# Two mixture-of-experts layers behind windowed attention on one core: the seam of the layers rearranged

## Chip, cores, metric

One core of a Trainium2 chip. The metric is the device time of one execution in microseconds, as the median of several runs. Traces come from one profiled execution. Engines: PE (TensorE), DVE (VectorE), ACT (ScalarE), POOL (GpSimd), SP (SyncE, which here only issues DMAs).

## What is computed

```
x = attention(q, k, v)                    # 2304 tokens x 512, windowed heads
for layer in (1, 2):                      # 8 experts, one expert for each token
    e    = argmax(x @ w_gate [+ modality_bias])
    gate = softmax(logits)[e]             # layer 1 also multiplies by a sigmoid
    x    = gate * (relu(x @ w1[e]) @ w2[e])     # w1[e]: 512x1024, w2[e]: 1024x512
```

The second layer's expert of a token can be known only from the first layer's result for it.

## The kernel before

Attention runs first (lines up to 540). Each mixture layer then works in **slots**: a slot is 128 tokens of one expert. A float32 value is split into a float16 high and low part (`hi`, `lo`), so one product becomes three matmuls. A slot in `moe` is:

- `mm1`, twice 48 matmuls of 128 columns (`ph0`, `ph1`; `ph<-xT,wb`, L824), for the two halves of the hidden units; `hsplit` turns each half into `hh` (ACT, L832) and `hl` (DVE, L833);
- 24 matmuls of 512 columns (L891): 16 on `hh`, then 8 on `hl`, into `py` (in slots 0 and 1 into `pya0`, `pya1`);
- `post.out` of the slot before: ACT scales `py` into a tile `y` (layer 2: L1139) and POOL scatters it to `out` by an indirect DMA (L1140). Layer 2 has two such tiles, `y[s % 2]`, so slot 2 writes the tile of slot 0 again. `post.out(2, py)` stands at the start of slot 3, ahead of slot 3's `hsplit` on ACT.

Slots 0 and 1 use an expert that is guessed early, with rows gathered early (`xsA`). What comes after them is known when `sort` has counted the tokens of each expert. `sort` is a generator that is stepped from hooks: step 1 is a chain on DVE, step 2 two small matmul groups, steps 3 and 4 a chain on DVE with parts on POOL and ACT (POOL makes `bs` and `bm`, DVE from them `ob` and `A`), step 5 the 54 small matmuls `pidx` (L690, L691), step 6 the row numbers `idx` (DVE cast, L695) and three gathers on POOL (L796, slots 2 to 4), step 7 the table `tab` of experts on DVE (L706 to L729), with the transposing DMAs `xT` (L803) and the loads of slot 3's weights (L88: eight pieces of 512 KB into `raw`, by SP, which must first read the table, L812), steps 8 and 9 the gates (`Bgb` on POOL, `pg` on PE, `flb`, `gsb`).

`first_splits(FIRST[0..3])` makes float16 weights `wb` of slot 3 out of `raw`: four parts, each an ACT instruction on 128x2048 (L96) and a DVE instruction (L101); each part, once split, lets SP load two pieces for slot 4 into the same place.

Nothing is scheduled by a program: the order on every engine is that in which the code issues. `plan` maps (slot, hook) to what is issued there: hook 0 is the slot's start, 1 within `ph0`, 2 behind it, 3 behind `hsplit(0)`, 4 within `ph1`, 5 behind `hsplit(1)`, 6 after 12 of the 24 wide matmuls, 7 the slot's end. Layer 2's sort (`so2`) also needs layer 1's last slot: `post1.out(None)`, eight transposes on PE with a DVE copy (`turn`), and `router(None)`.

In layer 1 `post1.out` writes `y16p[s % 2]`; the second of these tiles lies in `lotmp`, which earlier holds gathered rows that the DMA `xsA<-lotmp` reads. Its last 16 columns are cleared on POOL at L936, ahead of POOL's part of layer 1's sort.

Of the kernel before, what the change touches and what calls it, by code (L numbers as in the profile page):

```python
# [20 lines left out]
N, DM, E, F = 2304, 512, 8, 1024  # L21
# [3 lines left out]
P = 128  # L25
# [11 lines left out]
SX1, SX2, SW, SWR1, SWR = 2.0 ** 5, 2.0 ** 10, 2.0 ** 6, 2.0 ** 6, 2.0 ** 4  # L37
# [3 lines left out]
FIRST = ['B0:4 D0:4', 'B4:8 D4:8', 'B8:12 D8:12', 'B12:16 D12:16']  # L41
# [8 lines left out]
def fused(ctx, tc, qk, vw, wr1, w1a, w2a, mid, wr2, mbias, w1b, w2b, cf, c16, cbs, cms, cib, out, dbg=None):  # L50
    nc = tc.nc
# [71 lines left out]
    identh = const.tile([P, P], F16, name="identh")  # L123
# [18 lines left out]
    lg2 = const.tile([P, NSLOT, E], F32, name="lg2")  # L142
# [129 lines left out]
    with ExitStack() as actx:  # L272
# [208 lines left out]
        def stR(n):  # L481
# [3 lines left out]
            for j in range(5):  # L485
                c0 = 64 + P * j - (64 if odd else 0)
                for k, (a, w) in enumerate(((0, 0), (0, 1), (1, 0))):
# [10 lines left out]
                          lambda nm, sh, dt=F32: ap1.tile([P] + [CA1 if k < 0 else k for k in sh], dt, name=f"fs_{nm}"),  # L498
# [77 lines left out]
    m1 = ctx.enter_context(tc.tile_pool(name="m1", bufs=1))  # L576

    ctx.enter_context(tc.manual_schedule())
    pp = ctx.enter_context(tc.tile_pool(name="pp", bufs=1, space=PSUM))
    wb2 = m1.tile([P, 2, 8192], F16, name="wb2")  # L580
    xgb = [m1.tile([P, ROW], F16, name=f"xg{i}") for i in range(3)]
    xg2 = [m1.tile([P, ROW], F16, name=f"xgA{i}") for i in range(KA)]
    xsb = [m1.tile([P, 8, P], F16, name=f"xT{i}") for i in range(3)]
# [9 lines left out]
    vt, gt = nc.vector, nc.gpsimd  # L593
# [14 lines left out]
    def sort(nm, lg, nt, inv, fe, ea, tab, scale, og, extra, gscale, start):  # L608
# [5 lines left out]
        sh = [P, nt, E]  # L614
# [68 lines left out]
        for a in range(0, nt, ACH):  # L683
            n = min(ACH, nt - a)
# [45 lines left out]
        eql = T("eql" + nm, [NSLOT])  # L730
        v.tensor_scalar(eql, iota_t, nlast, None, op0=ALU.is_equal)
        start.eql, start.nlast = eql, nlast
        start.transpose(KA)
        start.weights(KE, range(0, 3), always=True)
        start.transpose(KA + 1)
        start.weights(KE, range(3, 8), always=True)
# [39 lines left out]
        g = m1.tile([P, NSLOT], F32, name=f"gs{nm}")  # L776
# [8 lines left out]
    def moe(w1, w2, tab, src, parts, post, start, wpair):  # L785


        xg, xs, regs, turns = {}, {i: xsA[i] for i in range(KA)}, {}, {}
        py = pp.tile([P, DM], F32, name="py", tag="py")
        pys = [pp.tile([P, DM], F32, name=f"pya{i}", tag=f"pya{i}") for i in range(KA)]  # L790
# [8 lines left out]
        def x_transpose(s):  # L799
            if s >= NSLOT:  # L800
                return
            g = xg.pop(s)
            nc.sync.dma_start(xsb[s % 3], g[:, 0:8 * P], transpose=True)  # L803
            xs[s] = xsb[s % 3]
            post.gathered(s, g)

        def weights(s, pieces=range(8), always=False):
            if s >= NSLOT:
                return
            if s not in regs:  # L810
                regs.pop(s - 2, None)
                regs[s] = (nc.sync.value_load(tab[0:1, 0, s:s + 1], min_val=0, max_val=E - 1),  # L812
                           None if always else nc.sync.value_load(tab[0:1, 1, s:s + 1], min_val=0, max_val=1))
            load_raw(w1, w2, regs[s][0], cond=regs[s][1], pieces=pieces)
# [20 lines left out]
        def slot(s):  # L835
# [40 lines left out]
            if s >= KA:  # L876
                x_transpose(s + 2)
# [20 lines left out]
                post.router(s - 2)  # L898
            hook(7)

        start.gather, start.transpose, start.weights, start.pys = gather, x_transpose, weights, pys
        start.first_splits = lambda o: splits(wpair[KE % 2], o, lambda k: weights(KE + 1, k))
        for s in range(NMIN):
            slot(s)
# [14 lines left out]
        return r  # L919

    class Start:
        def hook(self, s, k):
            for f in self.plan.get((s, k), ()):
                f()

    def run(gen, n=1):
        def go():
            for _ in range(n):
                next(gen, None)
        return go  # L930


    y16s = m1.tile([P, ROW], F16, name="y16")
    y16p = [y16s, lotmp[:, 0:520].bitcast(F16)]
    for t in (*y16p, xg2[0]):
        gt.memset(t[:, 2 * DM:], 0.0)  # L936
    wr2h = m1.tile([P, 2, 4, E], F16, name="wr2h")
    fes2 = first_expert("b", lg2[:, 0:1, :], lambda: pp.tile([P, E], F32, name="pfe2", tag="pyt"), fe2)
# [30 lines left out]
    class Start1(Start):  # L969
        def fields(self, g, inv, ex):  # L970
            self.g, self.inv = g, inv

            md = ex[:, 0]
            nmod = m1.tile([P, NSLOT], F32, name="nmod")
            gt.tensor_scalar(nmod, md, -1.0, 1.0, op0=ALU.mult, op1=ALU.add)
            bm = m1.tile([P, NSLOT, E], F32, name="bm", tag="tmp")
            sh = [P, NSLOT, E]
            gt.tensor_tensor(bm, mbt[:, 0, :].unsqueeze(1).to_broadcast(sh), nmod.unsqueeze(2).to_broadcast(sh), op=ALU.mult)
            gt.tensor_tensor(lg2, mbt[:, 1, :].unsqueeze(1).to_broadcast(sh), md.unsqueeze(2).to_broadcast(sh), op=ALU.mult)
            gt.tensor_tensor(lg2, lg2, bm, op=ALU.add)  # L980
# [19 lines left out]
    start1 = Start1()  # L1000

    class Post1:
# [38 lines left out]
        def router(self, s):  # L1041
            pl = pp.tile([P, E], F32, name="plg", tag="plg")
            yT = self.yT[0 if s is None else s % 2]
            k = 0
            for c in range(4):
                for a, b_ in ((c, 0), (c, 1), (4 + c, 0)):
                    nc.tensor.matmul(pl, yT[:, a, :], wr2h[:, b_, c, :], start=k == 0, stop=k == 11)
                    k += 1
            if s is None:
                tmp = m1.tile([P, NSLOT, E], F32, name="lgt", tag="tmp")  # L1050
                sh = [P, NSLOT, E]
                vt.tensor_tensor(tmp, pl.unsqueeze(1).to_broadcast(sh), start1.eql.unsqueeze(2).to_broadcast(sh), op=ALU.mult)
                vt.scalar_tensor_tensor(out=lg2, in0=tmp, scalar=1.0 / (SX2 * SWR), in1=lg2, op0=ALU.mult, op1=ALU.add)
            else:
                vt.scalar_tensor_tensor(out=lg2[:, s, :], in0=pl, scalar=1.0 / (SX2 * SWR), in1=lg2[:, s, :], op0=ALU.mult, op1=ALU.add)

    post1 = Post1()
    so1 = sort("a", lg1[:, :, 0:8], NT, None, fe1, early[0], tabs[0], 1 / (SX1 * SWR1), lg1[:, :, 8:16], [midf], SX2 / (SX1 * SW * SW), start1)
    fs2 = []

# [14 lines left out]
    def at(s, k, *f):  # L1075
        plan.setdefault((s, k), []).extend(f)
# [7 lines left out]
    for i in range(NSLOT - NMIN):  # L1084
        at(0, 3, lambda i=i: start1.zero(i))
    at(1, 5, lambda: start1.first_splits(FIRST[0]))
    at(2, 0, first_out(post1, start1, 0), lambda: start1.first_splits(FIRST[1]))
    at(2, 3, lambda: start1.first_splits(FIRST[2]))
    at(2, 5, first_out(post1, start1, 1), lambda: start1.first_splits(FIRST[3]))
    at(3, 7, start1.last)  # L1090
# [7 lines left out]
    py1 = moe(w1a, w2a, tabs[0], x_dram, (0, 1, 4, 5, 2, 3, 6, 7), post1, start1, wbuf)  # L1098
# [4 lines left out]
    ilast = m1.tile([P, 1], I32, name="ilast")  # L1103

    class Start2(Start):
        def fields(self, g, inv, ex):
            self.g = g
            oobf = m1.tile([P, NSLOT], F32, name="oobf")
            self.oob = m1.tile([P, NSLOT], I32, name="oob")
            gt.tensor_scalar(oobf, inv, float(OOB), None, op0=ALU.mult)  # L1110
            gt.tensor_copy(self.oob, oobf)
            for i in sorted(post2.rows):
                post2.index(i)
# [34 lines left out]

    start2, post2 = Start2(), Post2()
    so2 = sort("b", lg2, NSLOT, start1.inv, fe2, early[1], tabs[1], 1.0, None, [], 1 / (SX2 * SW * SW), start2)  # L1150
    plan = start2.plan = {}
    at(0, 0, lambda: post1.out(None, py1))
    at(0, 1, lambda: post1.transposes(None))
    at(0, 2, lambda: post1.router(None))
    at(0, 3, run(so2))
    at(0, 6, run(so2))
    at(0, 7, run(so2, 2))
    at(1, 5, run(so2, 2))
    at(1, 7, run(so2))
    at(2, 0, run(so2))  # L1160
    at(2, 2, run(so2))
    at(2, 0, lambda: start2.first_splits(FIRST[0]))
    at(2, 3, first_out(post2, start2, 0), lambda: start2.first_splits(FIRST[1]))
    at(2, 5, first_out(post2, start2, 1), lambda: start2.first_splits(FIRST[2]), lambda: start2.first_splits(FIRST[3]))
    at(3, 7, start2.last)
    py2 = moe(w1b, w2b, tabs[1], y_dram, range(8), post2, start2, [wb2, wbuf[1]])
    post2.out(None, py2)
# [60 lines left out]
def _build(arrays, dbg=None):  # L1228
    import concourse.bacc as _bacc
    nc = _bacc.Bacc("TRN2", target_bir_lowering=False, num_devices=1)  # L1230
    args = []
    for n in _ORDER:
        a = arrays[f"in_{n}"]
        args.append(nc.dram_tensor(f"in_{n}", a.shape, mybir.dt.from_np(a.dtype), kind="ExternalInput").ap())
    args.append(nc.dram_tensor("out_0", (N, DM), F32, kind="ExternalOutput").ap())
    d = {k: nc.dram_tensor(f"dbg_{k}", sh, dt, kind="ExternalOutput").ap() for k, (sh, dt) in (dbg or {}).items()}
    with tile.TileContext(nc) as tc:  # L1237
        fused(tc, *args, dbg=d)
    return nc
# [9 lines left out]
```

## Time and profile before

| | |
|---|---|
| median of 3 runs | 668.83 us (668.12 to 671.66) |
| profiled execution | 672.37 us, of which the trace's span is 670.5 |
| PE matmul busy | 595.0 us, 89% |
| DVE / ACT / POOL busy | 358.2 / 268.1 / 201.2 us |
| mean granted TensorE clock | 0.948 of full |

A busy PE includes matmuls at the lower clock. The first layer's slots begin at about 167 us, the second layer's at 442 us.

### The profile page before, as it was taken

Reading aid. Unit: us, or ns where it says so; the run is one execution under the profiler, and the core shown is the slowest. Engines: PE = TensorE matmul, PEld = TensorE weight load, DVE = VectorE, ACT = ScalarE, POOL = GpSimd, SP = SyncE. Lnnn points to the kernel's source line nnn. Section 1 sums busy time; section 2 is a strip of 40 time slices with the busy share of each in tenths; the row PEclk is TensorE's granted clock in tenths of the full one; section 3 lists DMA queues with packets and bytes.
Section 4 is the critical chain, followed back from the end, with each engine's and each line's share of the span. In section 5 each row is a group of like instructions: output and inputs, shape, how many; then the busy total and the mean of one; then the engine's idle time right before and its main releaser. Section 6 shows DMA issues by size and latency. Waiting matters only on the chain. (4 is left out here: it accounts for less than half of the span.)

```text
span 670.5 us, 19530 instructions
## 1 busy us (share of the span) xinstructions
PE 595.0 (89%) x7432; PEld 458.8 (68%) x7432; DVE 358.2 (53%) x656; ACT 268.1 (40%) x397; POOL 201.2 (30%) x327
## 2 busy tenths in 40 slices
PE   3888988942998899999999999979699999999994
PEld 2777877842865777777777768766558677686772
DVE  4599897758849535954849722239251110113560
ACT  4577776632355224823638411111332111113451
POOL 2467766715360211101102410003622122121320
PEclk9699998955899999999999999978989999999998
DMA  9999999996399965997877772200995252332921
GB/s 206 222 221 218 246 235 251 256 271 193 89 312 326 322 161 140 349 299 147 218 224 226 192 116 69 43 21 19 288 347 136 49 97 63 83 86 71 324 54 44
DMA packets 109573, 121.29 MB, mean 181 GB/s; under 512 B 73104, under 2 KB 77968, under 8 KB 108433
## 3 DMA queue, kind: packets, MB, share of 16 engines
q1 hardware_dynamic: 103776, 101.97, 59.9%
q0 software_dynamic: 5280, 17.13, 8.6%
q8 instruction: 62, 1.02, 0.6%
q10 hardware_dynamic: 400, 0.72, 0.5%
q14 instruction: 55, 0.44, 0.2%
HBM read 214.11 MB, written 18.22 MB: 346 GB/s over the span
## 5 line engine op out<-in xcount | busy, mean ns | idle before, releaser
L824 PEld LDWEIGHTS <-wb 128*128 128x128 f16 x4032 | 231.1, 99 | 15.5 <-issue 8.8
L824 PE MATMUL ph<-xT,wb 128*128 128x128 f16 x3648 | 210.2, 219 | 2.7 <-DMA xT<-xg 1.9
L833 DVE SCALAR_TENSOR_TENSOR hl<-ph,hh 128x512 f16<-128x512 f32 x84 | 57.7, 688 | 163.8 <-ACTq L847 158.1
L891 PE MATMUL py<-wb,hh 128*128 128x512 f16 x608 | 139.5, 382 | 4.3 <-ACT hh L832 4.3
L101 DVE SCALAR_TENSOR_TENSOR wb<-raw,wb 128x1024 f16<-128x1024 f32 (+1 forms) x80 | 103.0, 1325 | 27.2 <-ACT wb L96 27.0
L891 PEld LDWEIGHTS <-hh 128*128 128x128 f16 x672 | 64.4, 99 | 76.2 <-ACT hh L832 5.4
L832 ACT ACTIVATE hh<-ph 128x512 f16<-128x512 f32 x84 | 50.1, 596 | 139.0 <-PE ph L824 138.6
L96 ACT ACTIVATE wb<-raw 128x1024 f16<-128x1024 f32 (+1 forms) x80 | 87.0, 1133 | 18.8 <-DMA raw<-in_w1b 7.8
L891 PE MATMUL py<-wb,hl 128*128 128x512 f16 x304 | 73.0, 384 | 0.0
L891 PEld LDWEIGHTS <-hl 128*128 128x128 f16 x336 | 33.2, 99 | 40.9 <-issue 1.9
L1140 POOL DMA_INDIRECT out<-y,idx x18 | 18.0, 1001 | 124.5 <-ACTq L847 93.2
L420 PE MATMUL po<-v,pT 128*96 128x65 f32 x384 | 41.4, 262 | 0.4 <-DMA v<-in_vw 0.3
L420 PEld LDWEIGHTS po<-v,pT 128*96 128x96 f32 x384 | 38.2, 177 | 0.8 <-DMA v<-in_vw 0.7
L796 POOL DMA_INDIRECT xg<-x_dram,idxaa x23 | 27.2, 1183 | 29.0 <-DMA xT<-xg 19.9
L1139 ACT ACTIVATE y<-py,gsb 128x512 f32<-128x512 f32 x16 | 11.0, 687 | 57.4 <-PE py L891 57.4
L361 DVE TENSOR_REDUCE M<-ps 96x4 f32<-96x512 f32 x48 | 31.6, 679 | 4.0 <-PE ps L360 3.8
L359 PE MATMUL ps<-kh,qs 128*96 128x128 f16 x192 | 30.5, 235 | 3.3 <-ACT kh L315 3.0
L824 PE MATMUL ph<-xsA,wb 128*128 128x128 f16 x384 | 26.5, 238 | 7.7 <-issue 4.9
L359 PEld LDWEIGHTS <-qs 128*96 128x96 f16 x192 | 25.0, 135 | 12.0 <-DVE qs L340 6.9
L318 DVE SCALAR_TENSOR_TENSOR kl<-qk,kh 128x608 f16<-128x608 f32 x32 | 29.0, 909 | 5.6 <-ACT kh L315 5.3
L360 PE MATMUL ps<-kl,qs 128*96 128x128 f16 x192 | 30.1, 234 | 1.8 <-DVE kl L318 1.8
L355 PE MATMUL ps<-mS,identb 96*96 96x512 bf16 x48 | 20.4, 426 | 11.3 <-DMA mS<-in_cbs 8.8
(397 smaller groups left out, 746.9 us busy)
## 6 DMA issues: line engine op xcount, KB each, us to landing
raw<-in_w1a SPq DMA_DIRECT2D x95, 512.0 KB
raw<-in_w2a SPq DMA_DIRECT2D x92, 512.0 KB
raw<-in_w1b SPq DMA_DIRECT2D x75, 512.0 KB
raw<-in_w2b SPq DMA_DIRECT2D x72, 512.0 KB
qk<-in_qk SPq DMA_DIRECT2D x16, 608.0 KB
v<-in_vw SPq DMA_DIRECT2D x16, 390.0 KB
qk<-in_qk SPq DMA_DIRECT2D x16, 304.0 KB
y_dram<-y SPq DMA_DIRECT2D x11, 260.0 KB
```

Source lines behind the costliest of these rows:

```text
L96: nc.scalar.activation(wb[:, 0, s], raw[:, s], AF.Copy, scale=SW)
L101: nc.vector.scalar_tensor_tensor(out=wb[:, 1, s], in0=raw[:, s], scalar=SW, in1=wb[:, 0, s], op0=ALU.mult, op1=ALU.subtract)
L318: nc.vector.scalar_tensor_tensor(out=kls[n][:, h], in0=krs[n][:, h], scalar=SQK, in1=khs[n][:, h], op0=ALU.mult, op1=ALU.subtract)
L359: nc.tensor.matmul(ps[:, j, :], st, kh[:, h, QT * i:QT * i + 128], start=False, stop=False, skip_group_check=True)
L360: nc.tensor.matmul(ps[:, j, :], st, kl[:, h, QT * i:QT * i + 128], start=False, stop=j == 3, skip_group_check=True)
L361: nc.vector.tensor_reduce(out=Ms[n][:, 4 * g:4 * g + 4], in_=ps, axis=AX.X, op=ALU.max)
L420: nc.tensor.matmul(po[:, i, :], pT[:, NQ * h + i, :], v[:, h, i, :], start=True, stop=True)
L796: nc.gpsimd.indirect_dma_start(t, None, src, bass.IndirectOffsetOnAxis(start.idx[:, s:s + 1], 0))
L824: nc.tensor.matmul(ph[:, j, :], w[:, c, fs], xT[:, parts[c + i], :], start=k == 0, stop=k == 47, skip_group_check=True)
L832: nc.scalar.activation(hs, ph, AF.Relu)
L833: nc.vector.scalar_tensor_tensor(out=hl[:, 4 * g:4 * g + 4, :], in0=ph, scalar=0.0, in1=hs, op0=ALU.max, op1=ALU.subtract)
L891: nc.tensor.matmul(to, a, w, start=k == 0, stop=k == len(ops) - 1)
```

## The change

Nothing is computed differently; instructions move and one kind is replaced.

- Layer 2: `post1.transposes(None)` is issued in hook 0 of slot 0 and `router(None)` in hook 1, with step 1 of the sort right behind it, ahead of the slot's `hsplit`. The router's update touches only the 10 slots that can be the last one.
- Step 5 moves from hook 5 of slot 1 to hook 6, and step 9 from hook 2 of slot 2 to hook 5.
- Slot 2's rows are turned by eight PE transposes into PSUM and an ACT copy (`x_turned`), not by the DMA of L803.
- `first_splits(0)` comes at hook 3 of slot 2, the other three at hook 5; both `post2.out` of slots 0 and 1 move to hook 7, behind them.
- Layer 1: the clearing of the part of `lotmp` moves from the start to hook 0 of slot 2.

```diff
-        start.transpose(KA)
+        (start.turned if start.by_pe else start.transpose)(KA)
...
+        def x_turned(s):
+            g = xg.pop(s)
+            pt = pp.tile([P, 8, P], F16, name="pxt", tag="pyt")
+            for c in range(8):
+                nc.tensor.transpose(pt[:, c, :], g[:, c * P:(c + 1) * P], identh)
+            nc.scalar.copy(xsb[s % 3], pt)
+            xs[s] = xsb[s % 3]
+            post.gathered(s, g)
...
-    for t in (*y16p, xg2[0]):
+    for t in (y16s, xg2[0]):
         gt.memset(t[:, 2 * DM:], 0.0)
...
-    at(2, 0, first_out(post1, start1, 0), lambda: start1.first_splits(FIRST[1]))
+    at(2, 0, first_out(post1, start1, 0), lambda: start1.first_splits(FIRST[1]), lambda: gt.memset(y16p[1][:, 2 * DM:], 0.0))
...
-    at(0, 0, lambda: post1.out(None, py1))
-    at(0, 1, lambda: post1.transposes(None))
-    at(0, 2, lambda: post1.router(None))
-    at(0, 3, run(so2))
+    at(0, 0, lambda: post1.out(None, py1), lambda: post1.transposes(None))
+    at(0, 1, lambda: post1.router(None), run(so2))
     at(0, 6, run(so2))
     at(0, 7, run(so2, 2))
-    at(1, 5, run(so2, 2))
+    at(1, 6, run(so2, 2))
     at(1, 7, run(so2))
     at(2, 0, run(so2))
-    at(2, 2, run(so2))
-    at(2, 0, lambda: start2.first_splits(FIRST[0]))
-    at(2, 3, first_out(post2, start2, 0), lambda: start2.first_splits(FIRST[1]))
-    at(2, 5, first_out(post2, start2, 1), lambda: start2.first_splits(FIRST[2]), lambda: start2.first_splits(FIRST[3]))
+    at(2, 3, lambda: start2.first_splits(FIRST[0]))
+    at(2, 5, run(so2), *(lambda i=i: start2.first_splits(FIRST[i]) for i in (1, 2, 3)))
+    at(2, 7, first_out(post2, start2, 0), first_out(post2, start2, 1))
```

ACT in slot 2 of layer 2 before, from the second copy of `idx` on; `y_0` and `y_1` are the two result tiles, `pya` and `py` their sources:

```order
L696 COPY idxfb<-pidx 128x27
L741 ACTIVATE dlb<-dlb 128x216
L96 ACTIVATE wb_2779<-raw 128x2048
L775 COPY flb<-pg 128x108
L832 ACTIVATE hh<-ph_9311 128x512
L1139 ACTIVATE y_0_8800<-pya_8803,gsb 128x512
L96 ACTIVATE wb_2779<-raw 128x2048
L832 ACTIVATE hh<-ph_9443 128x512
L1139 ACTIVATE y_1_8801<-pya_8804,gsb 128x512
L96 ACTIVATE wb_2779<-raw 128x2048 x2
L906 TENSOR_LOAD tab_2801
L1139 ACTIVATE y_0_8800<-py,gsb 128x512
```

The same place on ACT with the change:

```order
L812 COPY xT_2799<-pxt 128x1024
L741 ACTIVATE dlb<-dlb 128x216
L841 ACTIVATE hh<-ph_9298 128x512
L96 ACTIVATE wb_2779<-raw 128x2048
L841 ACTIVATE hh<-ph_9372 128x512
L775 COPY flb<-pg 128x108
L96 ACTIVATE wb_2779<-raw 128x2048 x3
L1153 ACTIVATE y_0_8800<-pya_8803,gsb 128x512
L1153 ACTIVATE y_1_8801<-pya_8804,gsb 128x512
L915 TENSOR_LOAD tab_2801
L1153 ACTIVATE y_0_8800<-py,gsb 128x512
```

The results of slots 0 and 1 now stand behind all four weight parts, and the second use of `y_0` follows the first directly.

SP before, from the end of layer 1 on (`ISA` rows set registers):

```order
L907 UNCONDITIONAL_BRANCH x10
L803 DMA_TRANSPOSE xT_2799<-xg_2794 128x8x128
L812 TENSOR_LOAD tab_2801
L812 ISA x2
L88 ISA
L88 DMA raw<-in_w1b 128x1024
```

SP with the change:

```order
L916 UNCONDITIONAL_BRANCH x10
L821 TENSOR_LOAD tab_2801
L821 ISA x2
L88 ISA
L88 DMA raw<-in_w1b 128x1024
```

The transposing DMA ahead of the table's reading is gone.

POOL before, ahead of layer 1's sort (`bsa` and `bma` are its part of steps 3 and 4):

```order
L936 MEMSET y_2810 128x16
L936 MEMSET lotmp 128x16
L936 MEMSET xgA_2795 128x16
L653 TENSOR_SCALAR bsa<-slots_77,ha 128x27
L654 TENSOR_TENSOR bsa<-bsa,slots_77 128x27
```

POOL with the change:

```order
L947 MEMSET y_2810 128x16
L947 MEMSET xgA_2795 128x16
L653 TENSOR_SCALAR bsa<-slots_77,ha 128x27
L654 TENSOR_TENSOR bsa<-bsa,slots_77 128x27
L655 TENSOR_SCALAR bma<-slots_77,ha 128x27
```

The clearing of `lotmp` has left this place.

## Rows read from the trace of the kernel before

**Rows 1.** The page, part 1: busy time, share of the span, instructions.

```profile
PE 595.0 (89%) x7432; PEld 458.8 (68%) x7432; DVE 358.2 (53%) x656; ACT 268.1 (40%) x397; POOL 201.2 (30%) x327
```

**Rows 2.** Timeline of PE: start, duration, line, tiles, count, [idle before, releaser].

```profile
462.07 0.18 PE L690 MATMUL pidx<-obpb,Ab 128*128 128x27 f16 x1
...
462.48 0.17 PE L690 MATMUL pidx<-obpb,Ab 128*128 128x27 f16 x1
...
465.06 5.16 PE L891 MATMUL pya<-wb,hh 128*128 128x512 f16 x16
...
473.84 2.85 PE L824 MATMUL ph<-xT,wb 128*128 128x128 f16 x48 [1.89 <-DMA xT<-xg]
...
486.28 3.59 PE L891 MATMUL py<-wb,hh 128*128 128x512 f16 x8 [3.43 <-ACT hh L832]
...
492.61 5.52 PE L824 MATMUL ph<-xT,wb 128*128 128x128 f16 x96
497.97 3.62 PE L891 MATMUL py<-wb,hh 128*128 128x512 f16 x16
501.42 1.89 PE L891 MATMUL py<-wb,hl 128*128 128x512 f16 x8
```

**Rows 3.** Busy time by stretch; the last three columns: PE clock, DMA share, GB/s.

```profile
486.00:490.00 4.00, 3.72 (x9) 1.34 (x10) 4.00 (x3) 3.36 (x4) 0.00 (x0) 0.50 1.05 408
...
493.00:500.00 7.00, 7.00 (x102) 5.93 (x100) 1.86 (x3) 1.74 (x3) 2.02 (x2) 1.00 1.02 394
```

**Rows 4.** Timeline of ACT, layer 2, slots 2 and 3.

```profile
486.12 0.68 ACT L1139 ACTIVATE y<-pya,gsb 128x512 f32<-128x512 f32 x1
...
489.24 1.91 ACT L96 ACTIVATE wb<-raw 128x2048 f16<-128x2048 f32 x1 [0.64 <-DMA raw<-in_w2b]
492.86 0.69 ACT L1139 ACTIVATE y<-py,gsb 128x512 f32<-128x512 f32 x1 [1.71 <-PE py L891]
```

**Rows 5.** Timeline of SP, layer 2: start and duration of issuing.

```profile
469.63 1.27 SPq L803 DMA_TRANSPOSE xT<-xg  x1
472.50 1.65 SPq L88 DMA_DIRECT2D raw<-in_w1b  x3
```

**Rows 6.** Timeline of DVE, layer 2, the row numbers and the table's last row.

```profile
465.64 0.17 DVE L695 CAST idxbb<-pidx 128x27 int32<-128x27 f32 x1
...
469.22 0.17 DVE L729 CAST tab<-swb 128x27 int32<-128x27 f32 x1
```

**Rows 7.** DMA issues of 484 to 486, 493 to 494.2, 505 to 506: us to landing.

```profile
out<-y,idx POOLq DMA_INDIRECT x1, 7.7
...
out<-y,idx POOLq DMA_INDIRECT x1, 6.8
...
out<-y,idx POOLq DMA_INDIRECT x1, 3.4
```

**Rows 8.** Timeline of ACT, layer 1, start of slot 3.

```profile
207.02 0.69 ACT L1019 ACTIVATE y<-py,gsa 128x512 f16<-128x512 f32 x1 [4.00 <-DMA y_dram<-y]
207.75 2.00 ACT L96 ACTIVATE wb<-raw 128x1024 f16<-128x1024 f32 x2
```

**Rows 9.** Timeline of POOL, layer 2, the gate products.

```profile
473.05 4.12 POOL L766 TENSOR_TENSOR Bgb<-obb,g3b 128x729 f16<-128x729 f16 x3
```

**Rows 10.** Timeline of POOL, layer 1, ahead of the sort.

```profile
168.46 0.11 POOL L936 MEMSET lotmp<- 128x16 f16 x1 [4.79 <-DMA xsA<-lotmp]
```

**Rows 11.** Timeline of DVE, layer 1, slot 0.

```profile
170.05 0.67 DVE L678 TENSOR_TENSOR oba<-bma,pia 128x486 f16<-128x486 f32 x1 [1.92 <-POOL bma L656]
...
174.59 2.34 DVE L101 SCALAR_TENSOR_TENSOR wb<-raw,wb 128x1024 f16<-128x1024 f32 x2
...
177.45 0.17 DVE L695 CAST idxaa<-pidx 128x27 int32<-128x27 f32 x1
```

**Rows 12.** Timeline of ACT, layer 1, slot 0, the weight splits.

```profile
172.57 1.99 ACT L96 ACTIVATE wb<-raw 128x1024 f16<-128x1024 f32 x2
```

**Rows 13.** Timeline of PE, layer 1, end of slot 2.

```profile
205.83 0.46 PE L1047 MATMUL plg<-wr2h,yT 128*128 128x8 f16 x12 [1.51 <-DMA yT<-y]
```

More of the change, by code (lines that the diff above doesn't have):

```diff
@@ L899, in slot @@
             hook(7)
-        start.gather, start.transpose, start.weights, start.pys = gather, x_transpose, weights, pys
+        start.gather, start.transpose, start.turned, start.weights, start.pys = gather, x_transpose, x_turned, weights, pys
         start.first_splits = lambda o: splits(wpair[KE % 2], o, lambda k: weights(KE + 1, k))
@@ L921, in fused @@
     class Start:
+        by_pe = False
         def hook(self, s, k):
@@ L1049, in router @@
             if s is None:
[L1050 to L1053, printed above, removed]
+                n = NSLOT - NMIN + 1
+                tmp = m1.tile([P, NSLOT, E], F32, name="lgt", tag="tmp")[:, :n]
+                sh = [P, n, E]
+                vt.tensor_tensor(tmp, pl.unsqueeze(1).to_broadcast(sh), start1.eql[:, NMIN - 1:].unsqueeze(2).to_broadcast(sh), op=ALU.mult)
+                vt.scalar_tensor_tensor(out=lg2[:, NMIN - 1:], in0=tmp, scalar=1.0 / (SX2 * SWR), in1=lg2[:, NMIN - 1:], op0=ALU.mult, op1=ALU.add)
             else:
@@ L1105, in fused @@
     class Start2(Start):
+        by_pe = True
         def fields(self, g, inv, ex):
```

## The prediction

> **What bounds the kernel now.** I read the page first: PE is busy 89% of the span [rows 1], so a change is worth what it adds to or takes from PE's waits and PE's time at the lower clock. Then the timeline of PE over the second layer's first slots. From slot 3 on it has no gaps: 96 matmuls from 492.61, the wide ones from 497.97 [rows 2]. Before that PE loses time at four places: waits between the small matmuls, which spread the 54 of them from 462.07 to 465.06; 16 wide matmuls in 5.16 us at 465.06, where the same 16 take 3.45 at 497.97 (to 501.42); 1.89 us for slot 2's rows; and 3.43 us for `hh`, after which 16 wide matmuls take 6.33 (486.28 to 492.61) [rows 2]. The last loss is the clock: 0.50 granted (1.2 GHz) from 486 to 490, 1.00 (2.4 GHz) from 493 on [rows 3]. So **a wait of some 3.4 us costs PE another 6.33 - 3.45 = 2.9 us**, while the 1.89 us wait was followed by 48 matmuls at full rate (2.85 us, the pace of 96 in 5.52) [rows 2].
>
> Then the views of the engines that PE waits for. ACT's last weight part of slot 3 starts at 489.24, when its last two pieces have landed [rows 4]; DMA then carries about 400 GB/s [rows 3]. POOL's scatter of slot 0's result, issued in the window from 484, needs 7.7 us to land, the next one 6.8; one at 505 to 506, with no weights in flight, 3.4 [rows 7]. The first landed hardly before its tile was written again at 492.86, where ACT waited for PE alone [rows 4]. In layer 1's seam, where weights stream too, that same third result did wait, 4.00 us, for the first tile's transfer [rows 8]. This is the resource to watch.
>
> **Part 1, layer 2's sort.** Turning the last result at once moves 8 transposes past 32 matmuls on PE and leaves their number alone. It lets step 1 run earlier on DVE, but step 2 stays in hook 6, behind the same number of matmuls: I cost this at nothing, covered by slot 0's matmuls; without that cover its gain would be a few tenths. Step 5 goes behind 12 wide matmuls: 462.07 + 12 x 0.216 (3.45 / 16) = 464.66, and 54 small ones at 0.025 (17 intervals in 0.41 from 462.07 to 462.48 [rows 2]) end at 466.0. DVE's cast follows at about 466.3 in place of 465.64 [rows 6]: **0.65 later**. PE keeps its waits and probably its clock and is some 3 us earlier at the end of slot 1, but then waits for rows that are gathered 0.65 later.
>
> **Part 2, slot 2.** SP issued the rows' transposition at 469.63 [rows 5], so they had landed; now 470.3. Eight transposes (96 matmuls take 5.52: about 0.5, 0.9 at half clock) and ACT's copy of 128x1024, which the trace does not show: bounds 0.7 (one 128x512 result tile [rows 4]) and 1.4 (two); I take 1.2, nearer the row of twice its size. Slot 2 starts at about 472.3 instead of 473.84. Its gate products on POOL ended at 477.17 [rows 9]; the exponential they need now stands behind the copy, so 478 to 480. Then some 1.2 us of `pg`, 24 wide matmuls in 5.2, 8.1 at the lower clock: **slot 3 starts between 485 and 489, and its first half (5.4) ends by 491 to 494**. On PE alone that would be some 4 to 7 us gained.
>
> **Part 3, the weights and the results.** The table's last row ends 0.65 later, at 469.39 + 0.65 = 470.04 [rows 6]. SP no longer issues the transposition first; from that one's end (470.90) to the first weight (472.50) passed 1.6 us [rows 5], which I keep: first weight at 471.64, **0.86 earlier**. The freed transfer overlapped the weights by at most 473.84 - 472.50 = 1.3 us [rows 2, 5]; between 0 and 1.3 I take 0.4, since its data must have landed before PE started on them. The last pieces land 1.26 earlier: the last part starts at 488.0 and ends at 489.9 (1.91). Moving the four parts behind `hh` removes the 3.43 us wait of slot 2. But on ACT the result of slot 0 now stands behind the last part: 489.8 to 490.5; POOL's scatter starts at 490.6, not before 486.
>
> That scatter goes out while slot 4's eight pieces follow slot 3's. Its landing is between 3.4 and 7.7 us [rows 7]; I take 6.8, the nearer of the two that ran beside weight loads: 497.4. Only then may ACT write this tile again, for slot 2, and behind that instruction on ACT stand slot 3's two `hh`, while PE's wide matmuls of slot 3 need both `py` read and `hh`. ACT's next instruction came 0.73 after such a result (207.02, 207.75 [rows 8]); with 0.60 for `hh` and 0.1 at either end PE starts the wide matmuls at 497.4 + 0.1 + 0.73 + 0.6 + 0.1 = **498.9, against 497.97: 0.95 later**. PE will have waited some 5 to 8 us there, so I add the 2.9 for the clock. Sum at this seam: **+3.85**. The bounds of its terms: landing -3.4 / +0.9, the freed transfer -0.9 / +0.4, clock -2.9 / 0. Later slots have slack: the next scatter and slot 5's gather queue behind on POOL, two slots ahead of use.
>
> **Part 4, layer 1.** The clearing of `lotmp` made POOL idle 4.79 us [rows 10], and DVE's `ob` 1.92 behind it [rows 11]. Without it `ob` and `A` end 1.9 earlier, and DVE reaches its two low weight parts sooner; those need ACT's high parts, which end at 174.56 [rows 12], so the second low part (half of 2.34) ends near 175.8 instead of 176.93, and the cast comes about 1.0 earlier than 177.45 [rows 11]. Gathers, table and weights follow. At the end of slot 2 PE waits 1.51 for a transposition that queues behind these weights [rows 13]; it gains between 0 and 1.0: **-0.7**, nearer the end that the queue passes on. The clearing itself, 0.11 us on POOL, now lies beside matmuls.
>
> **Sum:** 672.37 + 3.85 - 0.7 = 675.5 for an execution like the profiled one. That lies 3.5 above the median of the runs shown; at the median, 668.83 + 3.15 = **672.0**. Half a per cent is 3.3 us, about what measurement of this kernel can tell from no change, so this forecast lies just inside it.
>
> **Rivals.**
>
> *A: the scatter does not queue behind the weights.* With 3.4 it lands at 494.0, the wide matmuls start at 495.5, 2.5 earlier; PE's wait is then 2 to 4 us, so the clock may or may not fall: -2.5 + 2.9 - 0.7 = -0.3, **668.5**, or -3.2, 665.6. Against it stand 7.7 and 6.8 under load [rows 7] and the 4.00 in layer 1 [rows 8].
>
> The Trainium skill, page "DMA: Bandwidth & Descriptors", section "Queues, rings and completion order", says that each DMA engine serves the queues with work in turn, a packet at a time. By that rule POOL's scatter would pass most of SP's queued weights, which is rival A and its 668.5. The 7.7 and 6.8 do not look like it, though a shared rate alone might explain part of them.
>
> *B: faster.* The weights come sooner than I say, since no transposition precedes them: eight pieces of 0.52 MB at 400 GB/s are 10.5 us. From 472 that is 482.5, with the remaining transposition about 484. The last part then ends at 486, the scatter starts at 486.7, and in a queue now shorter (3.4 to 4.5) lands by 491, before PE has finished slot 3's first half. Then nothing waits and slot 3 starts at 487 instead of 492.61: -5.6 - 0.7, **662.5**. It decides if the last part starts before about 485. Against: it started 16.7 us after the first weight [rows 4, 5].
>
> *C: slower still.* The scatter takes 7.7 or more, nothing is freed and layer 1 gives nothing: +0.95 + 0.9 + 0.4 + 2.9, **674.0**.
>
> **How the numbers follow.** Forecast with its own spread, C at its upper end (669.5 to 674): 0.75, of which I put 0.38 above the half per cent and 0.37 within, the point being so near it. A: 0.12, mostly within, 0.03 faster. B: 0.13. So faster 0.16, same 0.46, slower 0.38. The range reaches to A's lower value and to C, 665 to 674, and leaves out B and a little above C.
>
> **What would show it.** Right: ACT's second use of `y_0` waits several us for `out<-y`; PE's wide matmuls of slot 3 wait for `hh` and run at clock 0.50; no wait for `hh` in slot 2; the first weight of slot 3 issued about 0.9 earlier relative to slot 0's start; in layer 1 POOL's `bsa` starts as soon as DVE has `ha`. Wrong: a last weight part that starts before 486, or a scatter landing within 4 us under load, or slot 3 running without a gap.

## Result and profile after

The changed kernel took 675.38 us (median of 12 runs, 672.76 to 677.88), the kernel before 668.48 (12 runs, 667.48 to 672.42): ratio 1.0090, 95% interval 1.0067 to 1.0113. Slower, the way that was forecast (+3.15), but past the upper end of the range, 674. Two later measurements gave 1.0049 (1.0024 to 1.0075) and 1.0059 (1.0029 to 1.0089). A ratio is estimated from all runs, so it is not quite the quotient of the two medians.

The profiled execution took 672.76 us, only 0.4 more than that of before. So two questions stand: did the steps happen, and why do the medians differ by 6.9 where two traces differ by 0.4?

Page of the changed kernel, part 1:

```profile
PE 590.3 (88%) x7440; PEld 457.4 (68%) x7440; DVE 358.1 (53%) x656; ACT 268.8 (40%) x398; POOL 200.6 (30%) x327
```

PE is busy 4.7 us less than in [rows 1], yet the span is no shorter: what PE lost is waiting. Its timeline, layer 2, slots 2 to 4:

```profile
465.56 0.61 PE L811 MATMUL pxt<-identh,xg 128*128 128x128 f16 x8 [1.42 <-issue]
467.26 5.52 PE L833 MATMUL ph<-xT,wb 128*128 128x128 f16 x96 [1.10 <-ACT xT L812]
474.49 1.21 PE L773 MATMUL pg<-Bgb,Ab 128*128 128x81 f16 x27 [1.03 <-POOL Bgb L766]
475.54 3.62 PE L900 MATMUL py<-wb,hh 128*128 128x512 f16 x16
...
480.71 5.65 PE L833 MATMUL ph<-xT,wb 128*128 128x128 f16 x96
496.74 5.49 PE L900 MATMUL py<-wb,hh 128*128 128x512 f16 x16 [10.38 <-ACTq L856]
...
503.79 4.41 PE L833 MATMUL ph<-xT,wb 128*128 128x128 f16 x76
```

The waits of [rows 2] between the small matmuls and for `hh` are gone; ahead of slot 2 stand 1.42 and 1.10, ahead of the gates' `pg` 1.03, and slot 3 starts at 480.71. In place of the others is one of 10.38 us. Who makes it, in ACT's timeline (answers to [rows 4]):

```profile
484.70 1.91 ACT L96 ACTIVATE wb<-raw 128x2048 f16<-128x2048 f32 x1 [1.70 <-DMA raw<-in_w2b]
486.52 1.25 ACT L1153 ACTIVATE y<-pya,gsb 128x512 f32<-128x512 f32 x2
495.17 0.69 ACT L1153 ACTIVATE y<-py,gsb 128x512 f32<-128x512 f32 x1 [7.41 <-DMA out<-y,idx]
496.09 1.31 ACT L841 ACTIVATE hh<-ph 128x512 f16<-128x512 f32 x2 [0.23 <-ACTq L856]
```

ACT stands 7.41 us before slot 2's result, because the transfer of slot 0's result still reads the tile; slot 3's `hh` is behind it, and PE behind that. POOL's timeline, the DMA issue in 487 to 490 (landing), SP's first weight, and the clock of 497 to 500 (third column from the end):

```profile
488.04 1.86 POOL L1154 DMA_INDIRECT out<-y,idx  x1 [8.56 <-ACT y L1153]
```

```profile
out<-y,idx POOLq DMA_INDIRECT x1, 7.0
```

```profile
466.19 1.77 SPq L88 DMA_DIRECT2D raw<-in_w1b  x3
```

```profile
497.00:500.00 3.00, 3.00 (x8) 1.06 (x7) 1.47 (x4) 0.40 (x1) 1.60 (x2) 0.50 0.53 176
```

This is the forecast chain: results behind the last weight part, a scatter that takes 7.0, ACT held, PE's wide matmuls at 1.2 GHz (0.50).

I measure the **second seam** from PE's first instruction of layer 2 to slot 4's first matmul. Before: 442.39 to 503.15 = 60.76. After: 438.85 (eight transposes that now lead) to 503.79 = 64.94: **+4.18, forecast +3.85**. In layer 1, POOL's `bsa` now starts when DVE has `ha`:

```profile
164.83 0.38 POOL L653 TENSOR_SCALAR bsa<-slots,ha 128x27 f32<-128x27 f32 x1 [2.24 <-DVE ha L651]
```

and the **first layer**, from slot 0's first matmul to layer 2's first PE instruction, went from 442.39 - 167.24 = 275.15 to 438.85 - 166.21 = 272.64: -2.5, forecast -0.7. So the two traces differ little because four differences nearly cancel: -1.0 ahead of layer 1's slots, -2.5, +4.2 and -0.1 behind slot 4's start.

### The profile page after: what moved, and what is told of

The parts are those of the page before. It is cut to its first block, busy times and chain, and to the rows that moved or that the text cites. A ratio compares the mean times of both kernels' runs of the same rounds, so it can differ in the third digit from the quotient of the medians.

```text
span 671.0 us, 19550 instructions
## 1 busy us (share of the span) xinstructions
PE 590.3 (88%) x7440; PEld 457.4 (68%) x7440; DVE 358.1 (53%) x656; ACT 268.8 (40%) x398; POOL 200.6 (30%) x327
## 5 line engine op out<-in xcount | busy, mean ns | idle before, releaser
L842 DVE SCALAR_TENSOR_TENSOR hl<-ph,hh 128x512 f16<-128x512 f32 x84 | 57.7, 689 | 172.5 <-ACTq L856 163.0
L900 PE MATMUL py<-wb,hh 128*128 128x512 f16 x608 | 139.3, 383 | 10.4 <-ACTq L856 10.4
L406 PE MATMUL pst<-mt,msel 128*128 128x96 bf16 x192 | 30.4, 218 | 1.9 <-ACT mt L394 1.7
L409 ACT ACTIVATE pT<-pst 128x384 f32<-128x384 f32 x48 | 23.3, 487 | 18.6 <-PE pst L408 18.1
```

What stands on the lines that cost most here:

```text
L406: nc.tensor.matmul(ps[:, j, :], msel[:, typ, j, :], mt[:, g, :], start=j == 0, stop=False, skip_group_check=True)
L842: nc.vector.scalar_tensor_tensor(out=hl[:, 4 * g:4 * g + 4, :], in0=ph, scalar=0.0, in1=hs, op0=ALU.max, op1=ALU.subtract)
L900: nc.tensor.matmul(to, a, w, start=k == 0, stop=k == len(ops) - 1)
```

## Experiments

Every kernel's trace in the two lengths just defined, and its ratio to the kernel before (runs on the same chip). `e1_same_again` and `e4_same_third` are the changed kernel unedited, `e3_before_a` and `e3_before_b` the kernel before unedited; each of the others is described below with its edit:

| kernel | layer 1, slot 0 | layer 2, first | slot 4 | first layer | second seam | ratio (95%) |
|---|---|---|---|---|---|---|
| before, as shown | 167.24 | 442.39 | 503.15 | 275.15 | 60.76 | |
| e3_before_a | 163.62 | 437.03 | 498.10 | 273.41 | 61.07 | |
| e3_before_b | 164.56 | 439.16 | 496.82 | 274.60 | 57.66 | |
| e2_clear_only | 166.84 | 441.13 | 499.71 | 274.29 | 58.58 | 0.9976 (0.9948 to 1.0005) |
| e4_clear_again | 170.97 | 443.72 | 501.68 | 272.75 | 57.96 | 0.9990 (0.9964 to 1.0015) |
| e2_sort_only | 165.56 | 441.31 | 498.86 | 275.75 | 57.55 | 0.9989 (0.9961 to 1.0018) |
| e2_turn_only | 167.69 | 445.53 | 507.36 | 277.84 | 61.83 | 0.9992 (0.9964 to 1.0020) |
| e1_old_plan | 165.72 | 438.13 | 495.81 | 272.41 | 57.68 | 0.9927 (0.9904 to 0.9949) |
| changed, as shown | 166.21 | 438.85 | 503.79 | 272.64 | 64.94 | 1.0090 (1.0067 to 1.0113) |
| e1_same_again | 166.84 | 439.59 | 504.63 | 272.75 | 65.04 | 1.0049 (1.0024 to 1.0075) |
| e4_same_third | 168.81 | 444.00 | 508.95 | 275.19 | 64.95 | 1.0059 (1.0029 to 1.0089) |
| e2_no_clear | 168.29 | 443.50 | 508.54 | 275.21 | 65.04 | 1.0100 (1.0066 to 1.0135) |
| e4_no_clear_again | 163.93 | 441.85 | 506.40 | 277.92 | 64.55 | 1.0110 (1.0066 to 1.0153) |
| e3_no_loads | 168.68 | 441.75 | 503.28 | 273.07 | 61.53 | 1.0034 (1.0009 to 1.0060) |
| e1_third_tile | 165.67 | 437.36 | 492.85 | 271.69 | 55.49 | 0.9928 (0.9902 to 0.9954) |
| e1_out_ahead | 164.56 | 436.16 | 491.44 | 271.60 | 55.28 | 0.9924 (0.9895 to 0.9953) |
| e3_both | 167.93 | 440.23 | 493.53 | 272.30 | 53.30 | 0.9929 (0.9897 to 0.9961) |

**Is it the tile? Three ways to take the wait away, and the changed kernel beside them.**

A third result tile (`e1_third_tile`, in a part of `lotmp` that layer 2 leaves free):

```diff
-        y = [m1.tile([P, DM], F32, name=f"y2_{i}", tag=f"y{i}") for i in range(2)]
+        y = [m1.tile([P, DM], F32, name=f"y2_{i}", tag=f"y{i}") for i in range(2)] + [lotmp[:, 520:]]
...
-            y = y16s[:, 0:2 * DM].bitcast(F32) if s is None else self.y[s % 2]
+            y = y16s[:, 0:2 * DM].bitcast(F32) if s is None else self.y[s % 3]
```

> The changed kernel, with a third result tile for layer 2, so that slot 2's result does not write the tile of slot 0. Nothing else moves. Theory W: the 7.4 us wait of ACT for out<-y is gone; slot 2's result can follow slot 1's at 487.8, hh of slot 3 starts 0.73 later, PE's wide matmuls of slot 3 start at about 489.2 in place of 496.74, 7.5 earlier, and slot 4 starts 7.5 to 9 earlier (a wait of some 2.8 us is left, so the lower clock may stay): about 667, between 665.5 and 668.5. Rival V, or that another wait stands close behind the tile's (slot 4's weights, say): 672 to 676.

The results ahead of three weight parts (`e1_out_ahead`):

```diff
-    at(2, 5, run(so2), *(lambda i=i: start2.first_splits(FIRST[i]) for i in (1, 2, 3)))
-    at(2, 7, first_out(post2, start2, 0), first_out(post2, start2, 1))
+    at(2, 5, run(so2), first_out(post2, start2, 0), first_out(post2, start2, 1), *(lambda i=i: start2.first_splits(FIRST[i]) for i in (1, 2, 3)))
```

> The changed kernel, with the results of slots 0 and 1 and their scatters ahead of the last three weight parts instead of behind them (still behind the gates). Theory W: the first scatter starts at about 479.5 instead of 488.0 and lands by 487.2 even at 7.7 us; the two results take 1.4 us of ACT where it waits for weights anyway; PE's wide matmuls of slot 3 start at about 488.6 instead of 496.74: about 667, between 665 and 669. Rival: the two results wait for the gates and hold up the weight parts and with them everything by 2 to 3 us: 670 to 672. Rival V: 674 to 676.

Part 3 undone, and step 9 of the sort with it (`e1_old_plan`):

```diff
-    at(2, 3, lambda: start2.first_splits(FIRST[0]))
-    at(2, 5, run(so2), *(lambda i=i: start2.first_splits(FIRST[i]) for i in (1, 2, 3)))
-    at(2, 7, first_out(post2, start2, 0), first_out(post2, start2, 1))
+    at(2, 2, run(so2))
+    at(2, 0, lambda: start2.first_splits(FIRST[0]))
+    at(2, 3, first_out(post2, start2, 0), lambda: start2.first_splits(FIRST[1]))
+    at(2, 5, first_out(post2, start2, 1), lambda: start2.first_splits(FIRST[2]), lambda: start2.first_splits(FIRST[3]))
```

> The changed kernel, with Part 3 undone: weight parts, results of slots 0 and 1 and the last step of the sort at the hooks of slot 2 where they were before. The earlier sort, the rows turned by TensorE and the later clearing in layer 1 stay. Theory W: the seam loses its 4.2 us again, and keeps at most the 0.86 of the earlier first weight: 668 to 671, at or a little below the kernel before's time plus 1. Rival X (TensorE's turning or the new place of the sort costs the time): 674 to 676.

Unedited (`e1_same_again`):

> The changed kernel once more, nothing edited, so that the runs beside it have it on the same chip. The two profiled executions differ by 0.4 us, the two medians by 6.9. Theory W (result tile: ACT waits for the scatter of slot 0's result before it can write slot 2's, and the seam is 4.2 us longer, in every execution): about 675, a wait of 6 to 9 us of ACT for out<-y in the trace, second seam (slot 0's first matmul to slot 4's first) 64 to 66 us. Rival V (most of the difference of the medians lies where the change has nothing, in the attention or in the first layer): a trace with a second seam of about 61 to 62 us, or an end in which another stretch than the second seam is longer than in the kernel before.

ACT and PE with the third tile:

```profile
485.01 1.25 ACT L1153 ACTIVATE y<-pya,gsb 128x512 f32<-128x512 f32 x2
486.15 0.69 ACT L1153 ACTIVATE lotmp<-py,gsb 128x512 f32<-128x512 f32 x1
...
493.55 0.69 ACT L1153 ACTIVATE y<-py,gsb 128x512 f32<-128x512 f32 x1 [5.22 <-DMA out<-y,idx]
```

```profile
487.66 3.63 PE L900 MATMUL py<-wb,hh 128*128 128x512 f16 x16 [2.37 <-ACTq L856]
```

ACT no longer waits before slot 2's result, PE waits 2.37 in place of 10.38 and its 16 wide matmuls keep the full rate (3.63). The seam fell from 65.04 in the unedited kernel beside it to 55.49, the median from 673.31 to 664.57 us. With the results ahead, the last wait for the tile is 1.07:

```profile
475.83 1.27 ACT L1153 ACTIVATE y<-pya,gsb 128x512 f32<-128x512 f32 x2 [1.81 <-POOL gsb L779]
...
484.68 0.69 ACT L1153 ACTIVATE y<-py,gsb 128x512 f32<-128x512 f32 x1 [1.07 <-DMA out<-y,idx]
```

Both remedies went the way of theory W and past its ranges (665.5 to 668.5 and 665 to 669 expected, 664.6 and 664.2 measured, the kernel before at 671.0). So did the old plan (668 to 671 expected, 665.2 measured): what is left of the change without Part 3 gains more than I had allowed. Rival X is out, and by its own sign rival V too: the unedited kernel's seam is 65.04 again.

**Does the scatter wait for the weights?** In layer 2 the first parts load nothing for slot 4 (`e3_no_loads`, which leaves out part of the work):

```diff
-    at(2, 3, lambda: start2.first_splits(FIRST[0]))
-    at(2, 5, run(so2), *(lambda i=i: start2.first_splits(FIRST[i]) for i in (1, 2, 3)))
+    FIRST2 = [o.split()[0] for o in FIRST]
+    at(2, 3, lambda: start2.first_splits(FIRST2[0]))
+    at(2, 5, run(so2), *(lambda i=i: start2.first_splits(FIRST2[i]) for i in (1, 2, 3)))
```

> The changed kernel without the first eight loads of slot 4's weights in layer 2 (slot 4 then computes with slot 3's weights, so this one leaves out part of the work), so that the scatter of slot 0's result has no weights beside it. Theory L (the scatter lands late because it shares the DMA engines with the weights): it lands 2.7 to 3.4 us after its issue in place of 7.0, ACT's wait of 7.4 falls to 3.1 to 4, slot 3's wide matmuls start 3.5 to 4.3 earlier, second seam 59 to 61.5, ratio to the kernel before about 0.998 to 1.001. Rival (issue and completion on POOL's queue take the 7 us by themselves): wait still 6.5 to 7.5, second seam 65.

ACT and PE without those loads:

```profile
489.49 1.25 ACT L1153 ACTIVATE y<-pya,gsb 128x512 f32<-128x512 f32 x2
494.74 0.69 ACT L1153 ACTIVATE y<-py,gsb 128x512 f32<-128x512 f32 x1 [4.00 <-DMA out<-y,idx]
```

```profile
496.31 5.40 PE L900 MATMUL py<-wb,hh 128*128 128x512 f16 x16 [6.94 <-ACTq L856]
```

The wait fell from 7.41 to 4.00 and the seam by 3.4 (64.94 to 61.53): about half of the wait is the weights' doing, and the other half is what a scatter takes alone. That is theory L: the wait lies within its range and the other sizes just past theirs (the scatter lands after 3.7 us, the wide matmuls start 3.3 us earlier). The ratio, 1.0034, lies above the expected 1.001; its interval reaches there. Even so the seam is longer than the kernel before takes on the mean (59.2, below): part of the price is there without the loads. What the queues carried in the changed kernel, from 489 to 490, from 493 to 494 and from 493.5 to 493.75 (packets, MB, and the packets' time as a share of the 16 engines' span, which in these rows can pass 100%):

```profile
q1 hardware_dynamic: 102, 0.42, 104.2%
...
q1 hardware_dynamic: 109, 0.22, 59.8%
q0 software_dynamic: 45, 0.18, 46.0%
...
q0 software_dynamic: 16, 0.07, 64.8%
q1 hardware_dynamic: 16, 0.03, 35.1%
```

The scatter was issued at 488.04. From 489 to 493 every packet is one of SP's queue (q1); POOL's (q0) first show between 493.2 and 493.3, 5.2 us after the issue. Without the loads they first show 2.4 us after it. The Trainium skill, page "DMA: Bandwidth & Descriptors", section "Queues, rings and completion order", has each engine serve the queues that have work in turn, a packet at a time. From POOL's first packet on the rows agree with that: from 493.5 to 493.75 each queue has 16 packets. But about 2.8 of the 3.3 us by which the scatter lands later than without the loads pass ahead of that packet, while SP's queue alone is served; what holds POOL's first packet back there, no run here shows.

**Which part gains what?** Part 1 alone (`e2_sort_only`), and Part 2's turning of slot 2's rows alone (`e2_turn_only`; the router's update is cut to 10 slots in both):

```diff
-    at(0, 0, lambda: post1.out(None, py1))
-    at(0, 1, lambda: post1.transposes(None))
-    at(0, 2, lambda: post1.router(None))
-    at(0, 3, run(so2))
+    at(0, 0, lambda: post1.out(None, py1), lambda: post1.transposes(None))
+    at(0, 1, lambda: post1.router(None), run(so2))
...
-    at(1, 5, run(so2, 2))
+    at(1, 6, run(so2, 2))
```

> The kernel before with Part 1 alone: the last result turned at once, the sort's first step ahead of the activations, its small matmuls behind 12 wide ones. The second seam was 57.7 with old weight parts and both of the other edits, 3.1 less than before, and DVE's cast of the row numbers came 0.5 earlier after slot 0's start, not 0.65 later as forecast. Theory P (most of the 3.1 is the transposition's): second seam 60 to 60.5, ratio 0.999, a longer wait (4 to 6 us) for slot 2's rows on PE. Theory R (most is the sort's, whose waits on PE are gone): second seam 58 to 59, ratio 0.996.

```diff
-        start.transpose(KA)
+        (start.turned if start.by_pe else start.transpose)(KA)
```

> The kernel before with the rows of slot 2 turned by TensorE and nothing else (the sort, the weight parts, the results and the clearing as before; the table of the last result's update is cut to 10 slots). Theory P (the transposing DMA ahead of the weights costs more than the 0.86 us forecast: with the change the first weight was issued 27.4 us after slot 0's start in place of 30.1): first weight at 27.8 to 28.3, second seam 58.5 to 59.5, ratio 0.9965 to 0.998. Theory Q (as forecast, 0.86 and covered by hh's wait for weights): second seam 60 to 60.8, ratio 0.999 to 1.0.

Neither moves the time by itself by more than its interval (0.9989, 0.9992). PE's timeline, first of the sort alone, then of the turning alone, then of the old plan:

```profile
472.45 4.61 PE L824 MATMUL ph<-xT,wb 128*128 128x128 f16 x48 [5.62 <-DMA xT<-xg]
```

```profile
475.94 2.84 PE L833 MATMUL ph<-xT,wb 128*128 128x128 f16 x48 [1.10 <-ACT xT L812]
485.22 2.00 PE L773 MATMUL pg<-Bgb,Ab 128*128 128x81 f16 x27 [5.76 <-POOL Bgb L766]
```

```profile
473.73 2.00 PE L773 MATMUL pg<-Bgb,Ab 128*128 128x81 f16 x27 [3.71 <-POOL Bgb L766]
```

With the sort alone slot 1 is done sooner and PE waits 5.62 for the rows, as theory P had it, and the ratio is theory P's; the seam (57.55) is shorter than either theory's, but the kernel before takes as little in some executions (57.66, below). With the turning alone the rows come at once, but ACT's copy stands ahead of the exponential on which POOL's gate products hang, and `pg`, still ahead of slot 2's second half, waits 5.76. The exponential comes 475.79 - 445.53 = 30.3 us into the seam, against 469.86 - 442.39 = 27.5 before; and in this trace, that of the slowest of the 12 runs, the gate products take 6.17 us in place of 4.12 [rows 9], for a reason that no run shows. The first weight was issued 472.90 - 445.53 = 27.4 us into the seam, against 472.50 - 442.39 = 30.1: theory P's price for the transposition is right, but its seam did not come, and the ratio is theory Q's. In the changed kernel, with step 9 at hook 5, `pg` waits 1.03.

That the parts gain only together is not shown. The old plan has the new sort, turning and clearing and a ratio of 0.9927, but its seam (57.68) is that of the sort alone, and `pg` waits 3.71 there. Its first layer is the shorter one (272.41, against 275.75 and 277.84), and there only the clearing differs. The product of the single ratios is 0.9957 or 0.9971, by which of two measurements of the clearing alone (below) is taken, and with intervals of about 0.003 either way it is not told apart from 0.9927.

**Was the execution before a typical one?** The kernel before, twice more:

> The kernel before, unchanged, for a second trace. The second seam (slot 0's first matmul to slot 4's) took 60.8 in the profiled execution shown and 58.6 in the kernel that differs from it by the first layer's clearing alone, where no wide matmuls after the wait for hh ran at the lower clock. Theory B (the profiled execution shown was an expensive one, and the usual execution does not pay the lower clock there): second seam 58 to 59, so that the change's true price at this seam is about 6.4, not 4.2. Rival: 60.5 to 61, and the 58.6 was a lucky one. First seam 39 to 40.7 either way.

> The kernel before once more, a third trace, with the same question: second seam 58 to 59 by theory B, 60.5 to 61 by its rival; first seam 39 to 40.7.

PE's timeline in `e3_before_a` (61.07), then in `e3_before_b` (57.66):

```profile
459.68 5.14 PE L891 MATMUL pya<-wb,hh 128*128 128x512 f16 x16
...
468.35 2.85 PE L824 MATMUL ph<-xT,wb 128*128 128x128 f16 x48 [1.80 <-DMA xT<-xg]
...
481.59 3.60 PE L891 MATMUL py<-wb,hh 128*128 128x512 f16 x8 [4.12 <-ACT hh L832]
484.98 2.75 PE L891 MATMUL py<-wb,hl 128*128 128x512 f16 x8
```

```profile
461.38 3.61 PE L891 MATMUL pya<-wb,hh 128*128 128x512 f16 x16
...
469.92 4.48 PE L824 MATMUL ph<-xT,wb 128*128 128x128 f16 x48 [3.20 <-DMA xT<-xg]
...
482.79 1.90 PE L891 MATMUL py<-wb,hh 128*128 128x512 f16 x8 [2.25 <-ACT hh L832]
484.52 1.89 PE L891 MATMUL py<-wb,hl 128*128 128x512 f16 x8
```

One trace goes to theory B and one to its rival: the same program takes this seam in two ways. Either the lower clock falls on slot 1's wide matmuls (5.14) and again behind the wait for `hh` (granted clock 0.53 from 481.6 to 487 in `e3_before_a`), as in the execution that I read [rows 2]; or on slot 2's first half (4.48; granted clock 0.60 from 470 to 474 in `e3_before_b`) alone. Of five traces with this code at the seam (these three and the two with the clearing alone) two took 60.8 and 61.1 us, three 57.7 to 58.6; the mean of the five is 59.2. The five of the change's plan took 64.6 to 65.0, mean 64.9. **The seam's price is 5.7 on the mean**, between 4 and 7.

**What is the clearing worth?** Part 4 alone (`e2_clear_only`), and the change without it (`e2_no_clear`, the same edit backwards):

```diff
-    for t in (*y16p, xg2[0]):
+    for t in (y16s, xg2[0]):
...
-    at(2, 0, first_out(post1, start1, 0), lambda: start1.first_splits(FIRST[1]))
+    at(2, 0, first_out(post1, start1, 0), lambda: start1.first_splits(FIRST[1]), lambda: gt.memset(y16p[1][:, 2 * DM:], 0.0))
```

> The kernel before with Part 4 alone: the clearing of the part of lotmp moved to slot 2 of layer 1. The first seam (first layer, slot 0's first matmul to slot 3's) took 39.89 us in the profiled execution before, and 36.8 to 37.6 in five traces that have the later clearing. Theory G (the clearing is worth these 2.3 to 3.1 us in every execution): first seam 36.8 to 37.6, second seam as before (about 60.8), the whole 0.4 to 0.5% faster, ratio 0.9955. Theory F (the forecast's -0.7; the rest of the difference is the spread of executions): ratio 0.999, first seam 38.5 to 39.5.

> The changed kernel without Part 4: the clearing stands again ahead of the first layer's sort. Theory G: first seam 39 to 40 us, second seam 65, ratio to the kernel before 1.004 + 0.0045 = about 1.009 to 1.011. Theory F: ratio 1.005 to 1.008 and a first seam of no more than 38.5.

Both once more (`e4_clear_again`, `e4_no_clear_again`), with the changed kernel on the same chip:

> The changed kernel for the third time. From the traces so far: second seam 65.0 in three traces (one of them without the clearing), against 57.7, 58.6, 60.8 and 61.1 in four traces with the plan of before, mean 59.5, so +5.5; first seam 37.2 against 39.3, so -1.9 to -2.1 for the clearing. Sum +3.5, ratio 1.005 (theory N: 1.004 to 1.0065). Rival (the first measurement was right for the usual case): 1.0075 to 1.010. Second seam 64.5 to 65.5 by both.

> The changed kernel without Part 4, once more. Theory N: the ratio of the changed kernel of this call plus 0.002 to 0.004, about 1.008. Theory F (the clearing is worth the forecast's 0.7 and the rest was spread): plus 0.0005 to 0.0015. First seam 38.5 to 40 by N, under 38.5 by F.

> The kernel before with Part 4 alone, once more. Theory N: ratio 0.996 to 0.998 and a first seam of 36.8 to 38 (the 39.1 of the first trace was an unlucky one). Theory F: 0.9985 to 1.0 and a first seam of about 39 again.

The third measurement of the changed kernel, 1.0059, is theory N's. The first layer took 275.7 us on the mean of the seven traces with the early clearing and 272.9 on the ten with the late one: -2.8. The first seam took 39.1 on the mean of the seven and 37.6 on that of the ten. But single traces overlap: 39.11 and 39.31 are among the ten, 37.89 and 37.98 among the seven. Alone the clearing gave 0.24% and 0.10% (1.6 and 0.7 us), and out of the changed kernel 1.0110 - 1.0059 = 0.51% (3.4 us); `e2_no_clear`, 1.0100, had no changed kernel beside it. By the times theory F is nearer in the kernel before, theory N in the changed one, and the intervals allow either: **between 0.7 and 3.4 us, not settled closer**. One reason for the spread is in PE's timeline of `e4_no_clear_again`, where slot 3 came as early as 201.91, and in the changed kernel as shown:

```profile
221.78 1.01 PE L1049 MATMUL pyt<-identh,lotmp 128*128 128x128 f16 x8 [3.04 <-DVE fe_meb L187]
222.58 6.13 PE L900 MATMUL py<-wb,hh 128*128 128x512 f16 x16
```

```profile
222.25 0.61 PE L1049 MATMUL pyt<-identh,lotmp 128*128 128x128 f16 x8 [2.40 <-DVE fe_meb L187]
222.69 3.62 PE L900 MATMUL py<-wb,hh 128*128 128x512 f16 x16
```

What the first seam gains partly comes back two slots later as a wait for the guess of layer 2's first expert (`fe_meb`), and at 3.04 us it takes the clock with it (6.13 for what takes 3.62). In the ten traces with a first seam under 38 us this wait is 1.1 to 3.4 us; in five of the six with 39.1 or more it is at most 0.4.

**Both remedies together** (`e3_both`, the edits of the first two kernels):

> The changed kernel with both remedies, results ahead of the last three weight parts and a third result tile. With results ahead ACT still waited 1.07 us for the first scatter; with the third tile ACT's wait was gone and PE's was 2.37, most of it behind the last weight part. Theory W: the second seam goes from 55.3 to 54 to 55, ratio 0.990 to 0.992. Rival (what is left is the last weight part's data, not the tile): 55.3 and 0.992.

The seam is the shortest of all, 53.30, below theory W's range, but the time is no better than with one: 0.9929. Any of the four is some 5 us faster than the kernel before; which is best, these runs don't tell.

## Why the prediction was wrong

**Part 1.** Costed at nothing for the end; with the sort alone 0.9989 (0.9961 to 1.0018). But the cast was to come 0.65 later, and came 0.5 earlier (461.58 - 438.85 = 22.7 into the seam, against 465.64 - 442.39 = 23.2 [rows 6]): PE keeps no wait in slot 1 now. (From 462.07 to 462.48 lie 16 intervals, not 17; the 0.025 stands.)

```profile
461.58 0.18 DVE L695 CAST idxbb<-pidx 128x27 int32<-128x27 f32 x1 [0.67 <-PE pidx L691]
```

**Part 2.** Right in kind. The copy took 1.01 (1.2 taken); slot 2 ran without the wait for `hh`; slot 3 started 480.71 - 438.85 = 41.9 us into the seam, just ahead of the bounds of 42.6 to 46.6.

**Part 3.** The mechanism was right step by step. In us into the seam: last weight part 45.9 (forecast 45.6, by luck: the first weight came 2.8 earlier, not 0.86, and the last part started 18.5 after it, not 16.7); scatter issued 49.2 (48.2: it starts 1.5 after the result does, where I had 0.8); landing 7.0 (6.8); wide matmuls 57.9 (56.5), so 2.3 later than before where I had 0.95. The clock took 5.49 - 3.62 = 1.9 in place of 2.9. 2.3 + 1.9 = 4.2 against 3.85: the two terms were off by +1.35 and -1.0, so the close sum is luck in part.

**Part 4.** Right in sign; 0.7 is the lower end of what the runs give.

**The step that failed is a term of the sum: the +3.85 of the seam in "at the median, 668.83 + 3.15 = 672.0".** It is a difference from one execution, and I carried it to the median as if that execution's extra 3.5 us lay elsewhere. Of these, 1.6 us lie in this very seam: 60.76, against 59.2 on the mean of five traces of the same code. [rows 2] and [rows 3] show the lower clock behind the wait for `hh`; it goes on through the 8 matmuls on `hl`, which take 1.89 at the full rate:

```profile
489.67 3.11 PE L891 MATMUL py<-wb,hl 128*128 128x512 f16 x8
```

Three of the five traces do not pay these 2.9 us. The change pays its wait every time: 8.7 to 10.4 us in its five traces, with 5.4 to 6.5 for the 16 wide matmuls behind it. So the term is 5.7 in place of 3.85. Less 0.7 to 3.4 for Part 4 that gives +2.3 to +5.0; the three measured ratios give +6.0, +3.3 and +4.0 us. Of the 3.4 us between 672.0 and 675.38 the term accounts for 1.85, and Part 4 goes the other way. The rest stays open: in the later measurements the same pair came closer, and the first one's interval hardly meets the second's. Nor does the seam alone make an execution long: `e3_before_a` took 667.71 with a seam of 61.07. The upper end, 674.0 (rival C), added up late transfers, but had no term for a cheaper execution before.

**Rivals.** A (668.5) is out: beside the weights the scatter landed after 7.0, not 3.4, and without them the seam is 3.4 shorter. B needed a last part before 485 in the time of the execution before; it came at 442.39 + 45.9 = 488.2. Its idea, that nothing waits there, comes true with both remedies: in `e3_both` PE's wide matmuls of slot 3 start without a wait.

## What to carry to other kernels

When work is moved behind a late event, look for the buffer that the moved instruction writes, when it is written again, and which transfer must have read it by then; a spare tile or an issue a few instructions earlier was worth about 9 us here. Before a difference from one trace is added to a median, look at the seam in two or three traces: a clock that falls in some executions only is a term of its own. Here none of the three parts that ran alone (Part 3 did not) moved the time by more than its interval, while undoing Part 3 moved it by more than 1%: it can tell more to undo one part than to do one.

## What the hardware showed unexpectedly

- The start of layer 1's slot 0, ahead of which nothing runs that was edited (the clearing before came after it, at 168.46 [rows 10] against 167.24), lay between 163.6 and 171.0 us in the 17 traces: a spread of 7.4, more than the 5.7 of the seam.
- A wait does not always cost clock: 2.25 us for `hh` in `e3_before_b` was followed by wide matmuls at the full rate (1.90 for 8; granted clock 1.00 from 482.8 to 486), 4.12 in `e3_before_a` by 3.60 for 8.
- Without any load beside it, a scatter of 256 KB still held its tile for 494.74 - 491.01 = 3.7 us from its issue.

```profile
491.01 1.86 POOL L1154 DMA_INDIRECT out<-y,idx  x1 [8.57 <-ACT y L1153]
```
